# Three banks for the first layer, an ELU with two ScalarE passes, and scores from stacked rounded parts

## The chip, the core and the metric

The kernel runs on one core of one Trainium2 chip. The core has a matrix engine (TensorE, PE in the profile; PEld is its loading of weights), a vector engine (VectorE, DVE), an engine for activation functions (ScalarE, ACT), a general one (GpSimd, POOL), and SyncE (SP), which here issues nearly all DMAs. TensorE writes to PSUM, eight banks of 512 fp32 columns on 128 partitions; the other operands lie in SBUF. The metric is device microseconds of one launch, from inputs in HBM to the output in HBM.

## The reference

Causal block attention (8 batches, 8 heads, 576 positions, head size 64), then a dense layer pair with an ELU, then a soft mixture of eight experts over 32 slots. What matters here is the first two:

```python
scores = scale * np.matmul(q, k.transpose(0, 1, 3, 2))        # 576 x 576 for each of 64 heads
scores = np.where(block_i >= block_j, scores, -1e9)           # blocks of 64 positions
attn = np.exp(scores - np.max(scores, axis=-1, keepdims=True))
attn = attn / (np.sum(attn, axis=-1, keepdims=True) + 1e-09)
x = (attn @ v)                                                # 4608 tokens x 512
h = x @ w_in                                                  # 512 -> 2048
g = np.where(h > 0, h, np.exp(np.minimum(h, 0)) - 1)          # the ELU
y = g @ w_out                                                 # 2048 -> 512
# then: logits = y @ phi; softmax over tokens and over slots; experts on 32 slots; c @ slot_out
```

`w_out` is never applied to the 4608 tokens: it is folded into phi for the logits, and into the 32 slots for the experts.

## The kernel before, in words

**Attention** goes by pairs of heads: 32 pairs, four to a batch. `pair_load` and `pair_prep` bring queries and keys of a pair so that head 0 lies on partitions 0 to 63 and head 1 on 64 to 127, with the 64 head dimensions on the partitions. Pairs below `NTP` = 8 are transposed by TensorE out of a raw load (L516), later ones by VectorE (L525), after which GpSimd scales the queries (L531). `pair_scores` (L552) makes the scores in four fills of two PSUM banks: fill 0 the last 64 queries of both heads, fill 1 the two units of 512 keys, fill 2 those of 384 and 128, fill 3 those of 256. In fills 1 to 3 the two heads are fp32 products on 64 rows of the array each, side by side (L576); an fp32 product shows as two matmuls in the trace. Fill 0 of a later pair is a product on all 128 rows, of queries padded with zeros (L568). VectorE masks (L584) and takes the negated maximum (L587), ScalarE the exp with its sum (L590), GpSimd divides by the sum (L607). From pair 8 on, the weights are transposed by VectorE in 32 x 32 blocks (L689), with the blocks swapped through DRAM by DMAs (L717 to L721), and partly by TensorE through bank PTB (L700). The value products (L739) write banks PTB and PVB, and two copies bring them to the token ring `XR`.

**The first layer** goes by tiles of 128 tokens, 36 of them, each in four ranges of 512 hidden units. `tile_split` splits the tokens in a rounded part and the rest (L793, L795). A range is 12 products of 512 columns into one bank (L808 to L810: high x high, high x low, low x high, for four pieces of 128), alternately banks 0 and 1. ScalarE takes exp(h) into a buffer `E` (L813), VectorE min(e, 1) - 1 (L815), then the maximum with h into a slot of `g` (L818). From there VectorE's block transpose and DMAs turn `g` (`tile_turn`), and `tile_routing` makes the logits (L853) and sums the slots (L919).

**The order** is written by a list scheduler in the program (`Plan`). Every operation has an engine, an assumed duration, the buffers that it reads and writes, and a key; each engine takes the ready operation of the lowest key, at a time that the assumed durations give. DMAs share one modelled queue. The result is a fixed order for each engine. TensorE operations carry a mode (F full array, R row halves, C and D column parts), and a change costs the scheduler 0.13 us. At the end `tail` works the experts off, from pieces of 1 MB that are loaded into places that become free (`slots`).

## Time and profile before

| | us |
|---|---|
| median of 3 runs (lowest, highest) | 956.05 (955.30, 958.82) |
| the profiled execution | 955.77 |
| its span, first to last instruction | 954.0 |
| TensorE busy | 908.7 (95%) |
| VectorE busy | 675.9 (71%) |
| ScalarE busy | 439.4 (46%) |
| GpSimd busy | 272.6 (29%) |

Busy time is the union of an engine's instructions. Matmuls overlap in it, and their ends are modelled, so for TensorE the distance from one start to the next tells more. Idle time has a releaser: the instruction or DMA whose end let the engine go on. The kernel's shape in time: to 85 us attention alone and the splitting of the weights; from 86 to 866 us the first layer's tiles, with attention beside them to 779 us; then the experts and the output.

### The profile page before, as it was taken

How to read it: one execution, taken by the hardware profiler on the slowest of the kernel's cores; microseconds unless marked ns; L12 is line 12 of the kernel's file. 1: busy time of each engine (PE TensorE's matmuls, PEld its weight loads, DVE VectorE, ACT ScalarE, POOL GpSimd, SP SyncE). 2: the span in 40 equal slices, each digit the busy share in tenths (PEclk: the TensorE clock that was granted, in tenths of full speed). 3: DMA queues.
4: the chain of work that ended last, by engine and by line, in shares of the span. 5: the costliest groups of instructions: out<-in, count | busy, mean ns of one | idle time of the engine just before them, and what ended most of it. 6: DMA issues, size and time to landing. Idle time of an engine off the chain costs nothing.

```text
span 954.0 us, 19403 instructions
## 1 busy us (share of the span) xinstructions
PE 908.7 (95%) x6708; PEld 623.3 (65%) x6708; DVE 675.9 (71%) x1718; ACT 439.4 (46%) x1285; POOL 272.6 (29%) x428
## 2 busy tenths in 40 slices
PE   8889999999999999999999999999999999999992
PEld 6556777666666766676766666766776776766350
DVE  5887795668787887777888878887887844333160
ACT  5775655445445535444445445444444333322143
POOL 2863442133342332222323432332332210000000
PEclk9999999999999999999999999999999999999996
DMA  9846755647777785767677777667756498068969
GB/s 235 243 130 171 220 184 159 146 115 207 202 203 218 197 209 184 212 181 211 194 203 206 199 208 201 202 188 203 206 163 217 144 305 340 3 216 298 377 223 342
DMA packets 253217, 197.08 MB, mean 207 GB/s; under 512 B 183232, under 2 KB 206400, under 8 KB 250048
## 3 DMA queue, kind: packets, MB, share of 16 engines
q1 hardware_dynamic: 251920, 195.55, 69.1%
q8 instruction: 54, 0.88, 0.4%
q10 hardware_dynamic: 1200, 0.30, 0.1%
q14 instruction: 43, 0.35, 0.1%
HBM read 125.52 MB, written 70.25 MB: 205 GB/s over the span
## 4 chain that ended last, share of the span: by engine, by line
PE 74%; DVE 8%; DMA 7%; SPq 4%; ACT 2%; issue 2%; POOL 1%; ACTq 0%; DVEq 0%; POOLq 0%
PE ps L808 13%; PE ps L810 11%; PE ps L809 11%; PE ps L360 8%; PE ps L576 7%; PE ps L739 7%; SPq L355 4%; PE ps L919 3%; PE ps L568 2%; PE ps L853 2%; DMA att<-swapped 2%; DMA swapped<-att 2%; PE ps L767 2%; DVE base L587 2%; PE ps L460 1%
## 5 line engine op out<-in xcount | busy, mean ns | idle before, releaser
L808 PE MATMUL ps<-w,xhl 128*128 128x512 f32 x576 | 249.8, 434 | 7.8 <-DVE g L818 5.5
L607 POOL TENSOR_SCALAR att<-att,base 128x128 f32<-128x128 f32 (+4 forms) x288 | 181.0, 647 | 222.2 <-DVE base L603 151.0
L810 PE MATMUL ps<-w,xhl 128*128 128x512 f32 x576 | 226.8, 394 | 0.0
L809 PE MATMUL ps<-w,xhl 128*128 128x512 f32 x576 | 225.7, 392 | 0.0
L590 ACT ACTIVATE att<-ps,base 128x128 f32<-128x128 f32 (+4 forms) x288 | 157.4, 552 | 122.9 <-DVE base L587 121.0
L587 DVE TENSOR_REDUCE base<-ps 128x1 f32<-128x128 f32 (+4 forms) x288 | 135.7, 503 | 21.3 <-PE ps L572 12.2
L808 PEld LDWEIGHTS ps<-w,xhl 128*128 128x128 f32 x576 | 108.8, 189 | 52.0 <-issue 19.1
L813 ACT ACTIVATE xe<-ps 128x512 f32<-128x512 f32 x144 | 86.0, 600 | 115.0 <-PE ps L810 113.7
L810 PEld LDWEIGHTS ps<-w,xhl 128*128 128x128 f32 x576 | 108.1, 188 | 24.9
L336 ACT COPY att<-ps 128x128 f32<-128x128 f32 (+3 forms) x192 | 75.7, 434 | 95.8 <-PE ps L360 90.6
L809 PEld LDWEIGHTS ps<-w,xhl 128*128 128x128 f32 x576 | 108.9, 189 | 14.8
L815 DVE TENSOR_SCALAR xe<-xe 128x512 f32<-128x512 f32 x144 | 68.1, 473 | 67.0 <-ACT xe L813 65.6
L576 PE MATMUL ps<-att 64*128 64x128 f32 (+3 forms) x512 | 96.1, 468 | 1.0 <-ACT att L590 1.0
L360 PE MATMUL ps<-base,att 128*128 128x128 f32 (+1 forms) x496 | 83.2, 282 | 9.7 <-POOL att L607 8.5
L360 PEld LDWEIGHTS ps<-base,att 128*128 128x128 f32 (+1 forms) x496 | 58.0, 143 | 44.5 <-POOL att L607 17.6
L795 POOL TENSOR_TENSOR xhl<-xe,xhl 128x512 fp32r<-128x512 f32 x36 | 46.3, 1291 | 133.1 <-ACT xhl L793 127.0
L818 DVE TENSOR_TENSOR g<-xe,ps 128x512 f32<-128x512 f32 x108 | 73.3, 680 | 2.4
L689 DVE STREAM_TRANSPOSE att<-att 128x384 f32<-128x384 f32 x144 | 70.4, 507 | 5.3 <-POOL att L607 4.2
L739 PE MATMUL ps<-att 128*64 128x64 f32 (+4 forms) x864 | 71.9, 318 | 1.2 <-DMA att<-swapped 0.7
L576 PEld LDWEIGHTS ps<-att 64*128 64x128 f32 x512 | 42.0, 185 | 40.6 <-issue 14.1
L739 PEld LDWEIGHTS ps<-att 128*64 128x64 f32 x864 | 46.8, 137 | 32.3 <-issue 23.6
L826 DVE STREAM_TRANSPOSE g<-g 128x512 f32<-128x512 f32 x84 | 58.0, 695 | 1.7 <-DMA turned<-g 0.2
(134 smaller groups left out, 1115.1 us busy)
## 6 DMA issues: line engine op xcount, KB each, us to landing
turned<-g SPq DMA_DIRECT2D x60, 512.0 KB, 3.1
swapped<-att SPq DMA_DIRECT2D x24, 1024.0 KB, 4.6
g<-turned SPq DMA_DIRECT2D x120, 96.0 KB, 2.6
att<-in_moe_w_dram SPq DMA_DIRECT2D x11, 1024.0 KB, 11.8
att<-swapped SPq DMA_DIRECT2D x48, 192.0 KB, 3.9
att<-in_v_dram SPq DMA_DIRECT2D x64, 128.0 KB, 3.2
g<-in_moe_w_in_dram SPq DMA_DIRECT2D x16, 512.0 KB, 5.3
w_late<-in_moe_w_dram SPq DMA_DIRECT2D x8, 1024.0 KB, 6.9
```

Of the source, the lines that this page charges most:

```text
L336: nc.scalar.copy(o, i)
L360: mm(o, lhsT=i, rhs=f(IDN + base, n, base, base + n), start=True, stop=True, is_transpose=True)
L576: mm(pb(at((u, h)), P * (u + 1)), lhsT=f(qt + P * u, P, 64 * h, 64 * h + 64), rhs=f(kt, P * (u + 1), 64 * h, 64 * h + 64), start=True, sto ...
L587: add("DVE", 0.08 + wide(x) / 960, lambda e, x=x, c=c: nc.vector.tensor_reduce(out=f(c, 1), in_=pb(at(x), wide(x)), axis=AX.X, op=ALU.max, ...
L590: add("ACT", 0.50 + wide(x) / 1300, lambda e, x=x, c=c: nc.scalar.activation(f(pat(x, n), wide(x)), pb(at(x), wide(x)), AF.Exp, bias=f(c, ...
L607: add("POOL", (0.28 + wide(x) / 1050) * (1.3 if n < 8 else 1.0), lambda e, x=x, p=p: nc.gpsimd.tensor_scalar(out=f(p, wide(x)), in0=f(p, w ...
L739: mm(pb(o, w, 64 * h, 64 * h + 64), lhsT=f(vs + 320 * h + D * c, D), rhs=rhs(h), start=start, stop=stop)
L808: mm(pb(bank, 512), lhsT=fr(xh + P * kk, P), rhs=hi, start=(kk == 0), stop=False)
L809: mm(pb(bank, 512), lhsT=fr(xh + P * kk, P), rhs=lo, start=False, stop=False)
L810: mm(pb(bank, 512), lhsT=fr(xl + P * kk, P), rhs=hi, start=False, stop=(kk == 3))
L813: add("ACT", 0.48, lambda e: nc.scalar.activation(f(ee, 512), pb(bank, 512), AF.Exp), r=[("h", hb)], w=[("e", hb)], key=kr)
L818: add("DVE", 0.6, lambda e: nc.vector.tensor_tensor(out=f(g, 512), in0=f(ee, 512), in1=pb(bank, 512), op=ALU.max), r=[("e", hb), ("h", hb) ...
```

## The change

- **Third bank.** In tiles 6 to 33 (`THREE`) the ranges rotate through banks 0, 1 and PTB, and the exp is written into the range's slot of `g` in place of `E`. PTB is freed by letting TensorE's weight transposes use PVB, where the value products follow; their last 64 columns go to the end of the logits' bank (POST + 448), as five products of 64 columns.
- **ELU.** In tiles 6 to 29 (`RELU`) ScalarE takes relu(-h) and then exp(-that); VectorE takes max(e - 1, h) in one instruction, reading `g` and PSUM.
- **Scores.** From pair 9 on (`STACK`) queries and keys are split in a rounded part and the rest. X1 has the rounded queries on both halves of the partitions, X2 the queries' rest on the head's own half and zeros on the other, and Y the rounded keys on the own half and the keys' rest on the other. A unit is X1 by Y plus X2 by Y, both rounded products on the full array (L622 after). The own halves are written by ScalarE (L556, L558) and GpSimd (L567), the other halves come by DMA; the keys' rest is made by GpSimd first (L562). There is one place for queries, keys and stack where queries and keys had two, and masks of fill 2 are two memsets for four. Pair 8 now goes the raw way of the earlier pairs.
- **Tail.** Two of the pieces' places lie in the stack's area, one of them in parts, loaded by four DMAs.

```diff
...
+TLAG, LATE, NTP, JOINED, STACK = 2.5, 30, 8, 5, 9
+THREE = (6, 34)
+RELU = (6, 30)
...
+        if n == STACK:
+        for src, o, nm in ((q, RQ, "rq"), (k, RK, "rk")):
...
+        pair_split(n, key)
...
+    def pair_split(n, key):
+        add("POOL", 0.64, lambda e: nc.gpsimd.tensor_scalar(
+            out=f(QT[0], 512), in0=f(QT[0], 512), scalar1=SCALE, scalar2=0.0, op0=ALU.mult, op1=ALU.add), w=[("qt", 0)], key=key + 0.5)
+        for h in range(2):
+            here, there = (D * h, D * h + D), (D - D * h, P - D * h)
+            x1, x2, y, kl = X1[h], X2[h], Y[h], KL
+
+            def key_of(j):
+                return [("stack", h, j)]
+            add("ACT", 0.5, lambda e, x1=x1, here=here: nc.scalar.copy(st(x1, 512, *here), f(QT[0], 512, *here)),
+                r=[("qt", 0)], w=key_of(0), key=key + 1)
+            add("ACT", 0.5, lambda e, y=y, here=here: nc.scalar.copy(st(y, 512, *here), f(KT[0], 512, *here)),
+                r=[("kt", 0)], w=key_of(1), key=key + 1)
+            load(lambda x1=x1, there=there: st(x1, 512, *there, F32), lambda x1=x1, here=here: st(x1, 512, *here, F32), 200000,
+                 r=key_of(0), w=key_of(2), key=key + 2, lag=TLAG)
+            add("POOL", 1.35, lambda e, y=y, here=here: nc.gpsimd.tensor_tensor(
+                out=st(KL, 512, *here), in0=f(KT[0], 512, *here), in1=st(y, 512, *here, F32), op=ALU.subtract),
+                r=[("kt", 0)] + key_of(1), w=[("kl", h)], key=key + 2)
+            load(lambda y=y, there=there: st(y, 512, *there, F32), lambda here=here: st(KL, 512, *here, F32), 200000,
+                 r=[("kl", h)], w=key_of(3), key=key + 3, lag=TLAG)
+            add("POOL", 1.47, lambda e, x1=x1, x2=x2, here=here: nc.gpsimd.tensor_tensor(
+                out=st(x2, 512, *here), in0=f(QT[0], 512, *here), in1=st(x1, 512, *here, F32), op=ALU.subtract),
+                r=[("qt", 0)] + key_of(0), w=key_of(4), key=key + 3)
...
-        last = fill == 0 and n >= NTP
-        add("PE", (0.0 if last else 0.15) + cols / 600, sc, r=([("qb", s, 0), ("qb", s, 1)] if last else [("qt", s)]) + [("kt", s)], w=bkeys, key=key,
-            load=1.0, mode="F" if last else "R")
+        last = fill == 0 and n >= STACK
+        if n >= STACK and not last:
+            for h in range(2):
+                mine = [u for u, y in units if y == h]
+
+                def st_sc(e, h=h, mine=mine):
+                    for u in mine:
+                        for x, first in ((X1, True), (X2, False)):
+                            mm(pb(at((u, h)), P * (u + 1)), lhsT=st(x[h] + P * u, P), rhs=st(Y[h], P * (u + 1)), start=first, stop=not first)
+                add("PE", sum(2 * (0.016 + P * (u + 1) / 2400) for u in mine), st_sc, r=[("stack", h, j) for j in range(6)], w=[bkeys[h]], key=key)
+        else:
+            add("PE", (0.0 if last else 0.15) + cols / 600, sc, r=([("qb", s, h) for h in range(3)] if last else [("qt", one)]) + [("kt", one)],
+                w=bkeys, key=key, load=1.0, mode="F" if last else "R")
...
+            if n >= STACK and fill == 2 and x[0] == 2:
+                both = pb(at(x) + 256, 256, 0, 64).rearrange("p (a y) -> p a y", a=2)[:, :, 64:]
+                add("DVE", 0.14, lambda e, both=both: nc.vector.memset(both, MASKED), w=keys(x), key=key)
+            elif x != "b" and not (n >= STACK and fill == 2):
...
-            tb, tk = (PTB, "ptb")
+            tb, tk = (PVB, "pvb")
...
-            go(PTB, P, 0, lambda h: both[:, h, 0:P], True, True)
+            go(PVB, P, 0, lambda h: both[:, h, 0:P], True, True)
             for c in range(3):
                 w = P * (4 - max(c, 1))
-                go(PVB + 384 - w, w, c, lambda h: far(h, c), c == 0, False)
-                go(PVB + 384, 64, c, lambda h: both[:, h, P + 64 * c:P + 64 * c + 64], False, False)
-            go(PVB + 256, 192, 3, lambda h: both[:, h, 320:512], False, False)
-            go(PVB + 384, 64, 4, lambda h: both[:, h, 512:576], False, True)
-        add("PE", 3.0, pv, r=[("v", n % NV, j) for j in range(3)] + swap_keys(sl), w=["ptb", "pvb"], key=key, load=0.25, mode="C")
-        add(*evict(n, P), lambda e: copy(e, f(ring, P), pb(PTB, P)), r=["ptb"], w=[("xr", p, b % 2, 0)], key=key)
-        add(*evict(n, 448), lambda e: copy(e, f(ring + P, 448), pb(PVB, 448)), r=["pvb"], w=[("xr", p, b % 2, 1)], key=key)
+                go(PVB + 512 - w, w, c, lambda h: far(h, c), c == 0, False)
+            go(PVB + 384, P, 3, lambda h: both[:, h, 320:448], False, True)
+            for c in range(5):
+                x = P + 64 * c if c < 3 else 64 * c + 256
+                go(POST + 448, 64, c, lambda h: both[:, h, x:x + 64], c == 0, c == 4)
+        add("PE", 3.0, pv, r=[("v", n % NV, j) for j in range(3)] + swap_keys(sl), w=["pvb", "pvx"], key=key, load=0.25, mode="C")
+        add(*evict(n, 512), lambda e: copy(e, f(ring, 512), pb(PVB, 512)), r=["pvb"], w=[("xr", p, b % 2, 0)], key=key)
+        add(*evict(n, 64), lambda e: copy(e, f(ring + 512, 64), pb(POST + 448, 64)), r=["pvx"], w=[("xr", p, b % 2, 1)], key=key)
...
+        three = THREE[0] <= i < THREE[1]
+        if three:
+            hb = (4 * i + r) % 3
+        if (i, r) == (THREE[0], 0):
+            handover([("h", 2)], ["ptb"])
-        bank, ee = H0 + 512 * hb, E + 512 * hb
+        bank, ee, ek = ((H0, H0 + 512, PTB)[hb], g, gk) if three else (H0 + 512 * hb, E + 512 * hb, ("e", hb))
...
-        add("ACT", 0.48, lambda e: nc.scalar.activation(f(ee, 512), pb(bank, 512), AF.Exp),
-            r=[("h", hb)], w=[("e", hb)], key=kr)
-        add("DVE", 0.335, lambda e: nc.vector.tensor_scalar(
-            out=f(ee, 512), in0=f(ee, 512), scalar1=1.0, scalar2=-1.0, op0=ALU.min, op1=ALU.add),
-            w=[("e", hb)], key=kr)
-        add("DVE", 0.6, lambda e: nc.vector.tensor_tensor(
-            out=f(g, 512), in0=f(ee, 512), in1=pb(bank, 512), op=ALU.max),
-            r=[("e", hb), ("h", hb)], w=[gk], key=kr)
+        if RELU[0] <= i < RELU[1]:
+            add("ACT", 0.58, lambda e: nc.scalar.activation(f(ee, 512), pb(bank, 512), AF.Relu, scale=-1.0),
+                r=[("h", hb)], w=[ek], key=kr)
+            add("ACT", 0.55, lambda e: nc.scalar.activation(f(ee, 512), f(ee, 512), AF.Exp, scale=-1.0), w=[ek], key=kr)
+            add("DVE", 0.68, lambda e: nc.vector.scalar_tensor_tensor(
+                out=f(g, 512), in0=f(ee, 512), scalar=-1.0, in1=pb(bank, 512), op0=ALU.add, op1=ALU.max),
+                r=[ek, ("h", hb)], w=[gk], key=kr)
+        else:
+            add("ACT", 0.48, lambda e: nc.scalar.activation(f(ee, 512), pb(bank, 512), AF.Exp),
+                r=[("h", hb)], w=[ek], key=kr)
+            add("DVE", 0.335, lambda e: nc.vector.tensor_scalar(
+                out=f(ee, 512), in0=f(ee, 512), scalar1=1.0, scalar2=-1.0, op0=ALU.min, op1=ALU.add),
+                w=[ek], key=kr)
+            add("DVE", 0.6, lambda e: nc.vector.tensor_tensor(
+                out=f(g, 512), in0=f(ee, 512), in1=pb(bank, 512), op=ALU.max),
+                r=[ek, ("h", hb)], w=[gk], key=kr)
...
-        slots = [(flat(PT + PIECE * j), att) for j in range(10)]
+        slots = [(flat(PT + PIECE * j), att) for j in range(8)]
+        slots += [(lambda: renew("qk", F32, 1)[:, 0:PIECE].rearrange("p (c d) -> p c d", d=512), qkk), (lambda: parted, qkk + att)]
...
+                if o is not parted:
+                    nc.sync.dma_start(out=o.rearrange("p (c f) d -> p c (f d)", f=2) if wide else o,
+                                      in_=src.rearrange("(c p) d -> p c d", p=P))
+                    return
+                for c in range(4):
+                    part = src[P * (c // 2):P * (c // 2) + P, 512 * (c % 2):512 * (c % 2) + 512] if wide else src[P * c:P * c + P, :]
+                    nc.sync.dma_start(out=o[:, c, :], in_=part)
```

Three places in the order. First TensorE, fill 2 of a pair among first-layer products (L808 to L810 before, L862 to L864 after; `w` is the range's weights, `att` and `qk_late` hold queries and keys), before:

```order
L810 MATMUL ps<-w_70,xhl 128x512
L880 MATMUL ps<-base 128x128
L881 MATMUL ps<-base 128x32
L576 MATMUL ps<-att 128x384 x2
L576 MATMUL ps<-att 128x128 x2
L808 MATMUL ps<-w_71,xhl 128x512
L809 MATMUL ps<-w_71,xhl 128x512
L810 MATMUL ps<-w_71,xhl 128x512
L360 MATMUL ps<-base 128x128
```

and after:

```order
L862 MATMUL ps<-w_71,xhl 128x512
L863 MATMUL ps<-w_71,xhl 128x512
L864 MATMUL ps<-w_71,xhl 128x512
L622 MATMUL ps<-qk_late_2028 128x384 x2
L622 MATMUL ps<-qk_late_2028 128x128 x2
L862 MATMUL ps<-w_68,xhl 128x512
L863 MATMUL ps<-w_68,xhl 128x512
L864 MATMUL ps<-w_68,xhl 128x512
L369 MATMUL ps<-base 128x128
```

Two fp32 units of both heads have become, for one head, two rounded products of 384 and two of 128; the other head's stand a few products on.

Second ScalarE, at fills 2 and 3 of a pair (L590 and L638 are the scores' exp, L813 the ELU's), before:

```order
L590 ACTIVATE att,base<-ps,base 128x384
L590 ACTIVATE att,base<-ps,base 128x128 x2
L813 ACTIVATE xe<-ps 128x512 x2
L590 ACTIVATE att,base<-ps,base 128x256 x2
L813 ACTIVATE xe<-ps 128x512
L793 CAST xhl<-xe 128x512
L590 ACTIVATE att,base<-ps,base 128x576
```

and after:

```order
L870 ACTIVATE att<-att 128x512
L638 ACTIVATE att,base<-ps,base 128x384
L638 ACTIVATE att,base<-ps,base 128x128 x2
L868 ACTIVATE att<-ps 128x512
L556 CAST qk_late_2028<-att 64x512
L558 CAST qk_late_2028<-att 64x512
L638 ACTIVATE att,base<-ps,base 128x256 x2
```

The ELU has its two passes (L868 from PSUM, L870 in place), and two casts of the next pair's stack (L556, L558) stand ahead of fill 3's exps; two more follow.

Third GpSimd, from a pair's queries to its weights (L607 and L655; the 384, 128 and 256 columns are the second half), before:

```order
L607 TENSOR_SCALAR att<-att,base 128x576
L607 TENSOR_SCALAR att<-att,base 128x512 x2
L528 TENSOR_SCALAR base<-att 64x64 x2
L531 TENSOR_SCALAR att<-att 128x512
L607 TENSOR_SCALAR att<-att,base 128x384 x2
L607 TENSOR_SCALAR att<-att,base 128x128 x2
L607 TENSOR_SCALAR att<-att,base 128x256 x2
L795 TENSOR_TENSOR xhl<-xe,xhl 128x512
```

and after:

```order
L536 TENSOR_SCALAR att<-att 64x64 x2
L548 TENSOR_SCALAR att<-att 128x512
L655 TENSOR_SCALAR att<-att,base 128x576
L655 TENSOR_SCALAR att<-att,base 128x512 x2
L567 TENSOR_TENSOR qk_late_2028<-att,qk_late_2028 64x512
L562 TENSOR_TENSOR qk_late_2028<-att,qk_late_2028 64x512 x2
```

Between a pair's two halves of weights now stand the four subtractions of the next pair's stack (the fourth, L567, is the next row), and the second half comes behind them.

## Rows read from the trace of the kernel before

**Rows 1.** The page, part 1: busy us, share of the span, instructions.

```profile
PE 908.7 (95%) x6708; PEld 623.3 (65%) x6708; DVE 675.9 (71%) x1718; ACT 439.4 (46%) x1285; POOL 272.6 (29%) x428
```

**Rows 2.** Windows: stretch, length, busy us (instructions), TensorE clock, DMA share, GB/s.

```profile
165.00:866.00 701.00, 690.42 (x4936) 479.92 (x4924) 523.38 (x1371) 309.27 (x957) 194.24 (x329) 1.00 0.68 197
866.00:954.00 88.00, 66.37 (x575) 32.83 (x574) 26.17 (x52) 27.00 (x56) 0.00 (x0) 0.91 0.85 312
```

**Rows 3.** TensorE's waits, 200 to 760 us: us, times, longest us.

```profile
PE ps L808 <- DVE g L818: 5.5, 6, 2.0
...
PE ps L808 <- DVE att L818: 2.2, 3, 1.0
...
PE ps L739 <- DMA g<-turned: 0.4, 2, 0.2
```

**Rows 4.** TensorE's timeline: start us, us, line, operation, shape, count.

```profile
303.19 0.40 PE L810 MATMUL ps<-w,xhl 128*128 128x512 f32 x1
303.51 0.70 PE L576 MATMUL ps<-att 64*128 64x256 f32 x4
304.15 2.95 PE L739 MATMUL ps<-att 128*64 128x128 f32 x36
307.03 0.50 PE L808 MATMUL ps<-w,xhl 128*128 128x512 f32 x1
...
308.26 1.14 PE L568 MATMUL ps<-att,base 128*128 128x288 f32 x4
...
318.83 1.14 PE L576 MATMUL ps<-att 64*128 64x384 f32 x8
319.90 0.50 PE L808 MATMUL ps<-w,xhl 128*128 128x512 f32 x1
320.24 0.40 PE L809 MATMUL ps<-w,xhl 128*128 128x512 f32 x1
320.47 0.39 PE L810 MATMUL ps<-w,xhl 128*128 128x512 f32 x1
320.70 0.60 PE L360 MATMUL ps<-base,att 128*128 128x128 f32 x4
...
321.38 0.40 PE L809 MATMUL ps<-w,xhl 128*128 128x512 f32 x1
...
326.43 0.70 PE L576 MATMUL ps<-att 64*128 64x256 f32 x4
...
334.63 1.13 PE L576 MATMUL ps<-att 64*128 64x512 f32 x4
335.69 2.95 PE L739 MATMUL ps<-att 128*64 128x128 f32 x36
```

**Rows 5.** Instructions by line and form: busy us, mean ns, idle before and releasers.

```profile
L813 ACT ACTIVATE xe<-ps 128x512 f32<-128x512 f32 x144 | 86.0, 600 | 115.0 <-PE ps L810 113.7
...
L818 DVE TENSOR_TENSOR g<-xe,ps 128x512 f32<-128x512 f32 x108 | 73.3, 680 | 2.4
...
L815 DVE TENSOR_SCALAR xe<-xe 128x512 f32<-128x512 f32 x144 | 68.1, 473 | 67.0 <-ACT xe L813 65.6
...
L924 DVE SCALAR_TENSOR_TENSOR base<-base,ps 128x512 f32<-128x512 f32 x34 | 25.0, 737 | 13.4 <-PE ps L919 13.2
...
L793 ACT CAST xhl<-xe 128x512 fp32r<-128x512 f32 x36 | 22.0, 621 | 3.0 <-DVE xe L338 2.9
```

**Rows 6.** Timeline at 834 us, GpSimd and VectorE.

```profile
834.03 1.30 POOL L795 TENSOR_TENSOR xhl<-xe,xhl 128x512 fp32r<-128x512 f32 x1 [14.31 <-ACT xhl L793]
...
834.49 1.12 DVE L815 TENSOR_SCALAR xe<-xe 128x512 f32<-128x512 f32 x1 [2.50 <-ACT xe L813]
```

**Rows 7.** DMA issues: KB each, median us from issue to landing.

```profile
turned<-g SPq DMA_DIRECT2D x60, 512.0 KB, 3.1
...
g<-turned SPq DMA_DIRECT2D x120, 64.0 KB, 2.4
```

**Rows 8.** Waits of SyncE's queue: us, times, longest us.

```profile
SPq L355 <- DVE g L826: 32.8, 15, 6.5
```

More of the change, by code (lines that the diff above doesn't have):

```diff
@@ L258, in attention_moe_kernel @@
     SM = base.take(144)
-    QB = base.take(2 * P)
     XR = xe.take(4 * RING)
@@ L280, in attention_moe_kernel @@
     PB = aa.take(2 * PW[0] + PW[1])
+    X1, X2, Y, KL = (0, 512), (1024, 1536), (2048, 2560), 3072
+    qa.take(KL + 512 - qa.size)
     XH = xa.take(2 * 512)
@@ L391, in zero @@
                 nc.gpsimd.memset(f(PB + PW[0] * s + S, 64), 0.0)
-            nc.gpsimd.memset(f(QB, 2 * P), 0.0)
             for s in range(NV):
                 nc.gpsimd.memset(f(V + 640 * s, 640, 64, P).rearrange("p (h x) -> p h x", h=2)[:, :, 256:320], 0.0)
-        add("POOL", 0.9, zero, w=[("p", "b", s) for s in range(2)] + [("v", s, 2) for s in range(NV)] +
-            [("qb", s, h) for s in range(2) for h in range(2)], key=k0)
+        add("POOL", 0.9, zero, w=[("p", "b", s) for s in range(2)] + [("v", s, 2) for s in range(NV)], key=k0)
         raws = [(G + 1024 * j, 512, [("g", 2 * j), ("g", 2 * j + 1)]) for j in range(3)] + \
@@ L479, in pair_load @@
         b, p = divmod(n, 4)
-        s = n % 2
-        if n < NTP:
+        if n < STACK:
             for j, src in enumerate((q, k)):
@@ L531, in pair_prep @@
-        add("POOL", 0.55, lambda e: nc.gpsimd.tensor_scalar(
-            out=f(QT + S * s, 512), in0=f(QT + S * s, 512), scalar1=SCALE, scalar2=0.0, op0=ALU.mult, op1=ALU.add),
-            w=[("qt", s)], key=key + 1)
+                out=f(QB + P * s + D * h, D, D * h, D * h + D), in0=f(QT[0] + 512, D, D * h, D * h + D),
+                scalar1=SCALE, scalar2=0.0, op0=ALU.mult, op1=ALU.add), r=[("qt", 0)], w=[("qb", s, h)], key=key + 3.5)
+        if n == STACK:
+            handover([("stack", h, j) for h in range(2) for j in range(6)], [("qt", 1), ("kt", 1)] + [("raw", x, h) for x in range(3) for h in range(3)])
+            for h in range(2):
+                add("POOL", 0.4, lambda e, h=h: nc.gpsimd.memset(st(X2[h], 512, D - D * h, P - D * h, F32), 0.0), w=[("stack", h, 5)], key=key - 20)
@@ L564, in sc @@
         def sc(e):
-            if fill == 0 and n >= NTP:
+            if fill == 0 and n >= STACK:
                 for y in range(2):
@@ L1177, in attention_moe_kernel @@
     ev = []
+    before = None
     for n in range(NPAIR):
```

70 lines of the change are left out of this document (41 added, 29 removed).

## The prediction

> **What bounds the kernel now.** I read the views from the whole to the part. The busy totals first: TensorE works 908.7 of 954.0 us, VectorE 71%, ScalarE 46%, GpSimd 29% [rows 1]. Then two stretches: from 165 to 866 us TensorE is busy 690 of 701 us at a granted clock of 1.00, the higher of its two levels; the last 88 us are another regime, TensorE 66 us busy and the DMA engines at 0.85 [rows 2]. In the first stretch VectorE is the next engine, 523 of 701, ScalarE 309, GpSimd 194. Then the waits: between 200 and 760 us TensorE stood still mostly because a first-layer bank was not yet read, 5.5 + 2.2 us [rows 3]. So in the long stretch the time is TensorE's list, end to end, and only what shortens that list, or the 7.7 us of waits, counts. Busy time alone hides how it is spent, since ends of matmuls are modelled and overlap; I take distances from one start to the next in the timeline [rows 4].
>
> There a first-layer product of 512 rounded columns takes 0.23 us (320.24 to 320.47). Where a score block of two 64-row halves follows, the last product takes 0.32 (303.19 to 303.51): 0.09 more at the way in. The blocks themselves take 1.06 us (the two 512-column units, 334.63 to 335.69), 1.07 (384 and 128, 318.83 to 319.90) and 0.64 (256, 303.51 to 304.15). The first product behind one takes 0.34 (319.90 to 320.24): 0.11 more at the way out. Four 128-column transposes with the product behind them take 0.68 (320.70 to 321.38); less 0.23, that is 0.11 each, not a quarter of 0.23: so narrow a product does not go at its columns' price.
>
> **Scores.** Pairs 9 to 31, 23 of them, change. A pair now pays 1.06 + 1.07 + 0.64 = 2.77 us, and 3 x 0.09 on the way in, 3.04. The stacked form needs per unit two full-array rounded products: 4 of 512 columns, 4 of 384, 4 of 128, 4 of 256. No row shows 384 or 256 rounded columns: bounded below by columns (0.23 x 384/512 = 0.17 and 0.115), above by the 0.23 of a 512 product. I take the lower ends, because 512 columns are the same kind of product and nearest, and 0.11 for 128 from the transposes: 4 x (0.23 + 0.17 + 0.11 + 0.115) = 2.5 us. Saved 0.54 x 23 = 12.4 us. The way out of 0.11 goes too where a first-layer product follows, in half of the 69 blocks (38 of 77 in the order of before): 3.8 us. Value products and logits have array shapes of their own; where they stood beside a score block one change of shape served both, which now is paid to the first layer: I give 2 us back. The ends: every narrow product at 0.23 makes the pair 16 x 0.23 = 3.68, a loss of 0.64 x 23 = 14.7 us; columns alone (5,120 x 0.23/512 = 2.3) and a way out of 0.11 at every block a gain of 1.07 x 23 = 24.6 us.
>
> The 64-row blocks run both heads side by side. The Trainium skill (TensorEngine Tiling (Array Packing), Theoretical Speedup) gives up to a factor of two for that when a dimension is at most 64; by it alone, giving the packing up would cost another 2.77 us per pair, some 64 us, and the sum would be near 1003. The rows speak against it here: one fp32 512-column unit costs half of 1.06, two rounded products 0.46.
>
> **Third bank.** The 5.5 + 2.2 us of TensorE's waits for VectorE's last read of a bank [rows 3] should go between tiles 6 and 33. The stretch holds 34 tiles of four ranges, 5 us a range, and a bank will have two other ranges in which to be read, where it had one. I take 6 us; ends 0 and 7.7. Late next are the value products, which wait for the DMA that swaps the weights' blocks.
>
> **ELU.** Tiles 6 to 29, 96 ranges: ScalarE runs two passes (0.60 each by its Exp) where it ran one, +58 us; VectorE loses a pass of 0.47, and its last one becomes a form like the accumulation's 0.74 for 0.68: -0.41 x 96 = -40 us [rows 5]. The stacks add four casts of 0.62 a pair on ScalarE (+57 us) [rows 5] and four subtractions of 1.30 on GpSimd (+120 us) [rows 6]. ScalarE then has 309 + 115 = 424 of 701, GpSimd 314, VectorE 483: all under TensorE's 690, so I price them at nothing. The cover is the distance between a range and its bank's next use; gone, each range would pay the added pass, 0.6 x 96 = 58 us.
>
> **Stack.** Pair n+1's parts can be written only when pair n's last score block has read them, and its first stacked block waits for them, with the first layer queued behind it on TensorE. GpSimd takes the four subtractions in the order queries, keys, keys, queries, the first after two casts: the second half's keys are done after 2 x 0.62 + 3 x 1.30 = 5.1 us and then copied, 128 KB, for 2.4 to 3.1 us by the nearest copies [rows 7]: 7.5 to 8.2 us. In the order of after some 21 first-layer products (4.8 us), the 128-row block (1.1 at 308.26) and the value products (2.88, 304.15 to 307.03) stand between, 8.8 us; for other pairs as much in first-layer products. Before, the places stood 8.2 us apart (326.43 to 334.63) [rows 4]. So there is 0.6 to 1.3 us of room. The nearest wait, that of the value products for copied blocks, is 0.4 us in the whole stretch [rows 3]: I take 1 us, the upper end is a rival. GpSimd's weights of a pair's second half now stand behind the subtractions, so the value products' data come up to 5.2 us later; in the order the value products stand later too.
>
> **The rest.** Pair 8 goes the earlier pairs' way: ten transposes, +1.1 us. Value products get one more product of 64 columns for the same 1,600 columns: between 0 and 2.88/36 x 4 = 0.32 a pair, 7.4 us; equal columns are nearer, so 1 us. Transposes and values now share one bank; that they take turns there is as it was in the bank they leave. The tail (pieces in other places, one in four DMAs) moves with the last tile; between -2 and +2, taken 0.
>
> Sum: -12.4 - 3.8 + 2 - 6 + 1 + 1.1 + 1 = -17 us. The profiled execution took 955.77, so 939 (the median is 956.05, 0.3 more).
>
> **Rivals.** *The stack copy is late (slower).* The four copies stand in SyncE's one queue, among copies that wait for VectorE's transposes 2.2 us a time (32.8 us in 15) [rows 8]. With one such wait ahead of every pair's last copy, less 0.8 us of room, TensorE stands 1.4 us a pair: 23 x 1.4 = 32 us, so 971; from 17/23 = 0.74 us a pair the gain is gone. For it: path and room differ by little. Against: value products behind that same queue hardly wait now. 0.14.
>
> *VectorE takes TensorE's place (no change).* Beside a GpSimd subtraction the pass that goes took 1.12 us where its mean is 0.47 [rows 5, 6]. If 92 more subtractions hold other passes as long, VectorE has 92 x 0.65 = 60 us more, 543 of some 685, in bursts that TensorE waits for, and what the list loses comes back: 956. The Trainium skill (SBUF — State Buffer, Who interferes with whom) says that a VectorE instruction in a two-port mode, or with two SBUF inputs, excludes one of GpSimd for its whole length, and that one with at most one SBUF input outside those modes doesn't. The row agrees for the pass that goes; by that rule the new last pass, with one input in PSUM, is free, which no row here shows. 0.09.
>
> *More goes than I count.* The columns' end of the scores, -24.6, all 7.7 us of waits, and nothing new: 955.8 - 32 + 3 = 926. For it: every change of shape shows at both sides. Against: narrow products don't go by columns. 0.13.
>
> *It doesn't do what it says.* The waits for banks stay, because VectorE reads a bank as late as before (523 of 701 us busy), and value products and stacks pay 4 us more than taken: 955.8 - 12.4 - 3.8 + 2 + 1.1 + 6 = 949. 0.09.
>
> **Numbers.** Forecast 939, own range 931 to 947, 0.55; more gain 0.13; scores alone 0.09; no change 0.09; slower 0.14. Faster by over 0.5% (under 951.3; about what can be told from no change) takes the first three, 0.77. For eight in ten I go from 925, past the larger gain, to 954, which leaves out the slower case.
>
> **What would show it.** Right: TensorE's list from the first tile's steady pace to the last range about 17 us shorter, a stacked block of 512 columns with 0.23 us from start to start and no longer product before it, waits of the first layer for VectorE near zero, ScalarE up by 115 us and VectorE down by 40. Wrong: TensorE waiting at the first stacked block for a copy or for GpSimd, 128- and 256-column stacked products at 0.2 us, or VectorE's other passes longer. If TensorE's busy share falls below 0.95 in the long stretch, the forecast is wrong in kind and not in size.

## The result: slower by 1.4%

The changed kernel took 969.11 us (median of 4 runs, 967.96 to 971.93), the kernel before beside it 955.67 (954.39 to 958.82): ratio 1.0135, 95% interval 1.0105 to 1.0166. The forecast was 939, so it failed by 30 us and in sign. The profiled execution has a span of 967.6 us, 13.6 more than before.

The busy line of the page, and the two stretches (the second is again the tail):

```profile
PE 903.2 (93%) x6817; PEld 655.0 (68%) x6817; DVE 648.1 (67%) x1583; ACT 553.0 (57%) x1469; POOL 384.7 (40%) x519
```

```profile
165.00:880.00 715.00, 686.72 (x5060) 512.91 (x5058) 497.56 (x1236) 423.04 (x1141) 305.59 (x422) 1.00 0.74 209
880.00:967.00 87.00, 66.43 (x575) 32.84 (x574) 26.16 (x52) 26.83 (x56) 0.00 (x0) 0.91 0.87 315
```

Against [rows 1, 2]: ScalarE +114 us, GpSimd +112, VectorE -28 (counted: -40); the tail as long as before. All of the loss is in the long stretch, where TensorE works 4 us less in 14 us more: 0.96 of the time. TensorE's waits there (200 to 775 us) answer to [rows 3]:

```profile
PE ps L787 <- DMA att<-swapped: 9.8, 7, 3.3
PE ps L369 <- ACT base L951: 6.1, 4, 2.1
PE ps L622 <- DMA qk_late<-qk_late: 3.3, 3, 1.7
PE ps L862 <- DVE g L871: 2.0, 2, 1.2
PE ps L915 <- DMA g<-turned: 1.8, 3, 1.1
PE ps L787 <- DMA g<-turned: 1.2, 2, 0.7
```

The bank waits of the first layer (L862) fell from 7.7 us to 2.0: the third bank works. In their place, for one, the value products (L787) wait for the copy that brings the weights' swapped blocks back (att<-swapped), which was no row of weight before. The stack's own copies (L622 <- qk_late) take 3.3 us, not 32. The transposes' wait for ScalarE's exponential of the dispatch (L369 <- base L951) is new as well.

Where the time stands I took from the distance of each TensorE product's start to the next, from the first first-layer product to the last, summed by line; a wait counts to the product ahead of it (us):

| | before | after | no_copies (below) |
|---|---|---|---|
| first layer | 439.8 | 431.5 | 435.4 |
| value products, pairs 8 to 31 | 71.4 | 91.7 | 74.6 |
| score blocks, 128 columns and more | 80.6 | 76.8 | 74.8 |
| transposes | 54.8 | 57.3 | 54.2 |
| routing logits | 27.7 | 29.9 | 27.6 |
| all else | 105.8 | 106.9 | 104.7 |
| sum | 780.1 | 794.2 | 771.4 |

A value block without a wait takes 2.89 us (2.88 before, 4 products fewer). Of the 24 blocks' 91.7 us 22 are therefore lost, more than the whole loss of 14. By my sums these are three things. In 9 blocks TensorE stops behind the first four products until the swapped blocks have landed: 12.5 us (2.0 before). In two of them, pairs 14 and 22, the granted clock then stands at 0.50, the lower of its two levels, for 3.4 us, and the products come at half their pace: 3.0 us (none before).

```profile
381.30:384.70 3.40, 3.40 (x12) 1.60 (x14) 0.48 (x2) 0.00 (x0) 0.76 (x2) 0.50 0.61 159
579.30:582.70 3.40, 3.40 (x32) 2.68 (x28) 0.38 (x2) 0.58 (x1) 2.08 (x5) 0.50 0.39 105
```

And 6.5 us (0 before) are not the value products' at all: in 4 blocks they stand behind the last product, where a dispatch transpose waits for ScalarE, and count to the value block only because a wait counts to the product ahead of it. Pair 18:

```profile
479.21 2.96 PE L787 MATMUL ps<-att 128*64 128x128 f32 x40
484.29 0.33 PE L369 MATMUL ps<-base 128*128 128x128 f32 x1 [2.11 <-ACT base L951]
```

The longest stall for the swapped blocks, pair 14. First the place on TensorE:

```profile
377.22 0.40 PE L864 MATMUL ps<-w,xhl 128*128 128x512 f32 x1
377.54 0.44 PE L787 MATMUL ps<-att 128*64 128x128 f32 x4
381.28 4.42 PE L787 MATMUL ps<-att 128*64 128x384 f32 x36 [3.30 <-DMA att<-swapped]
385.62 1.08 PE L915 MATMUL ps<-g,base 128*32 128x128 f32 x32
```

8.08 us from 377.54 to 385.62 for a block of 2.89, 3.5 of them the stop and 1.7 the clock. Then SyncE's queue for the same pair, before and after (start, time of the issues, tiles, count; swapped<-att is the way out, att<-swapped the way back):

```profile
357.88 0.37 SPq L355 DMA_DIRECT2D swapped<-att  x1
358.30 3.06 SPq L355 DMA_DIRECT2D g<-turned  x4
361.40 0.42 SPq L355 DMA_DIRECT2D att<-in_k_dram  x1
362.34 3.28 SPq L355 DMA_DIRECT2D att<-swapped  x6
```

```profile
355.24 0.82 SPq L364 DMA_DIRECT2D qk_late<-qk_late  x1
356.11 2.94 SPq L364 DMA_DIRECT2D g<-turned  x6
359.14 1.11 SPq L364 DMA_DIRECT2D qk_late<-qk_late  x2
360.37 2.31 SPq L364 DMA_DIRECT2D att<-in_q_dram  x4
362.78 0.44 SPq L364 DMA_DIRECT2D turned<-g  x1
363.31 0.51 SPq L364 DMA_DIRECT2D att<-in_v_dram  x1
363.91 0.74 SPq L364 DMA_DIRECT2D swapped<-att  x1
364.75 1.61 SPq L364 DMA_DIRECT2D att<-in_v_dram  x2
366.45 4.30 SPq L364 DMA_DIRECT2D att<-in_k_dram  x4
370.80 2.84 SPq L364 DMA_DIRECT2D g<-turned  x6
373.74 0.37 SPq L364 DMA_DIRECT2D turned<-g  x1
374.15 3.18 SPq L364 DMA_DIRECT2D att<-swapped  x6
```

Read the gaps: after, there are none. GpSimd ended this pair's last weights at 357.3 (L655, 354.56 and 2.75 us) and VectorE their last block transpose at 358.8 (L737); the way out was issued at 363.91, behind the tile's blocks, stack copies and the next pair's queries, landed at 370.7, and the way back was issued at 374.15, behind keys and the tile's blocks. Before, the way back followed the way out's landing at once. Summed over the rows of 215 to 765 us, the queue's issues take 377 of 550 us before and 462 after: +57 for the 92 stack copies, and the loads beside them a little longer each.

### The profile page after: what moved, and what is told of

Same layout as the page of the kernel before. It is cut to its first block, busy times and chain, and to the rows that moved or that the text cites. A ratio compares the mean times of both kernels' runs of the same rounds, so it can differ in the third digit from the quotient of the medians.

```text
span 967.6 us, 20058 instructions
## 1 busy us (share of the span) xinstructions
PE 903.2 (93%) x6817; PEld 655.0 (68%) x6817; DVE 648.1 (67%) x1583; ACT 553.0 (57%) x1469; POOL 384.7 (40%) x519
## 4 chain that ended last, share of the span: by engine, by line
PE 59%; DMA 12%; DVE 7%; SPq 7%; ACT 6%; POOL 4%; issue 3%; ACTq 0%; DVEq 0%; POOLq 0%
PE ps L862 10%; PE ps L863 9%; PE ps L864 9%; PE ps L369 7%; SPq L364 7%; PE ps L787 5%; PE ps L622 4%; POOL att L655 3%; PE ps L981 2%; DMA att<-swapped 2%; PE ps L915 2%; DMA qk_late<-qk_late 2%; PE ps L816 2%; PE ps L611 2%; ACT att L638 2%
## 5 line engine op out<-in xcount | busy, mean ns | idle before, releaser
L655 POOL TENSOR_SCALAR att<-att,base 128x128 f32<-128x128 f32 (+4 forms) x288 | 179.7, 642 | 201.1 <-DVE base L651 113.8
L862 PE MATMUL ps<-w,xhl 128*128 128x512 f32 x576 | 246.6, 428 | 2.0 <-DVE g L871 2.0
L864 PE MATMUL ps<-w,xhl 128*128 128x512 f32 x576 | 226.6, 393 | 0.6 <-POOL xhl L844 0.6
L638 ACT ACTIVATE att<-ps,base 128x128 f32<-128x128 f32 (+4 forms) x288 | 157.5, 551 | 85.3 <-DVE base L635 76.0
L635 DVE TENSOR_REDUCE base<-ps 128x1 f32<-128x128 f32 (+4 forms) x288 | 139.4, 506 | 22.2 <-PE ps L607 10.5
L862 PEld LDWEIGHTS ps<-w,xhl 128*128 128x128 f32 x576 | 108.9, 189 | 33.7 <-issue 11.9
L864 PEld LDWEIGHTS ps<-w,xhl 128*128 128x128 f32 x576 | 108.1, 188 | 25.9 <-POOL xhl L844 1.2
L345 ACT COPY att<-ps 128x512 f32<-128x512 f32 (+3 forms) x184 | 73.0, 437 | 67.9 <-PE ps L369 62.5
L567 POOL TENSOR_TENSOR qk_late<-att,qk_late 64x512 fp32r<-64x512 f32 x46 | 59.0, 1283 | 90.7 <-ACT qk_late L556 64.3
L787 PE MATMUL ps<-att 128*64 128x128 f32 (+2 forms) x960 | 76.1, 312 | 11.5 <-DMA att<-swapped 9.8
L622 PE MATMUL ps<-qk_late 128*128 128x512 f32 (+3 forms) x368 | 77.6, 328 | 4.5 <-DMA qk_late<-qk_late 3.3
L369 PE MATMUL ps<-base,att 128*128 128x128 f32 x416 | 69.9, 280 | 10.6 <-POOL att L655 9.8
L787 PEld LDWEIGHTS ps<-att 128*64 128x64 f32 x960 | 50.3, 141 | 41.9 <-issue 30.9
L622 PEld LDWEIGHTS ps<-qk_late 128*128 128x128 f32 x368 | 61.3, 188 | 21.3 <-issue 6.9
L369 PEld LDWEIGHTS ps<-base,att 128*128 128x128 f32 x416 | 49.1, 143 | 39.2 <-POOL att L655 16.9
L737 DVE STREAM_TRANSPOSE att<-att 128x384 f32<-128x384 f32 x144 | 68.6, 503 | 1.0 <-POOL att L655 0.8
L562 POOL TENSOR_TENSOR qk_late<-att,qk_late 64x512 fp32r<-64x512 f32 x46 | 59.1, 1285 | 4.2 <-ACT qk_late L558 2.8
L638 ACT ACTIVATION_READ_ACCUMULATOR att<-ps,base 128x1 f32 x288 | 57.4, 199 | 0.0
```

The source lines that it names most:

```text
L345: nc.scalar.copy(o, i)
L369: mm(o, lhsT=i, rhs=f(IDN + base, n, base, base + n), start=True, stop=True, is_transpose=True)
L622: mm(pb(at((u, h)), P * (u + 1)), lhsT=st(x[h] + P * u, P), rhs=st(Y[h], P * (u + 1)), start=first, stop=not first)
L635: add("DVE", 0.08 + wide(x) / 960, lambda e, x=x, c=c: nc.vector.tensor_reduce(out=f(c, 1), in_=pb(at(x), wide(x)), axis=AX.X, op=ALU.max, ...
L638: add("ACT", 0.50 + wide(x) / 1300, lambda e, x=x, c=c: nc.scalar.activation(f(pat(x, n), wide(x)), pb(at(x), wide(x)), AF.Exp, bias=f(c, ...
L655: add("POOL", (0.28 + wide(x) / 1050) * (1.3 if n < 8 else 1.0), lambda e, x=x, p=p: nc.gpsimd.tensor_scalar(out=f(p, wide(x)), in0=f(p, w ...
```

## Experiments

Times are medians; "before" is what ran beside them, 955.2 to 957.0. Theory Q is SyncE's queue, G the subtractions on GpSimd, S ScalarE's second pass, B the bank that transposes and values share, T the copies' bytes, P the price of any other written-out order. The values' last 64 columns (line 795 of after) lie in the routing's bank, and a slot sum of one of the first five tiles fills all 512 columns of that bank; no dependence keeps the two apart, in the changed kernel neither. Its order does (pair 9's values from 262.4 us, VectorE's read of the sum at 261.8). In copies_act, after_lag, q_act, q_act_elu and no_copies one pair's values come over such a sum before it is read (no_copies: sum from 255.95, values from 256.95, the read at 259.95), in no_sub and rows3 a sum over values, so what they compute is not the reference's. It is one place near 250 us and every instruction is issued, so the times are read; with the two kept apart the order, and with it the time, would be another.

**Which part of the change.** Scores as before (the diff's other parts kept):

> Third bank, the value products' new places and the ELU as in the changed kernel; scores as before, so no casts, no subtractions, no stack copies. Theory Q (SyncE's queue is full, and the weights' copies for the value products wait in it): value products wait as little as before (2 to 4 us in all), the first layer keeps its 8 us: 946 to 950. Theory G (the subtractions on GpSimd hold up the weights): the same 946 to 950, since they are gone as well. Theory S (ScalarE's second pass of the ELU is what makes the chain late): 956 or more, with value products waiting.

Measured 964.68, ratio 1.0093 (1.0061 to 1.0126). Theories Q and G had 946 to 950 and fail; S had 956 or more with value products waiting, and 8 us are lost, 6 of them in value products. But bank_only below, without S's second pass, is as slow.

The stack copies on ScalarE:

```
-    r=key_of(0), w=key_of(2), key=key + 2, lag=TLAG)
+    r=key_of(0), w=key_of(2), key=key + 2, lag=TLAG, eng="ACT")
```

> The changed kernel with its 92 stack copies issued by ScalarE in place of SyncE; the same bytes at about the same times. Theory Q: 57 us of issue time leave SyncE's queue (92 x 0.62), the 20 us that TensorE loses in the value products fall under 8, 952 to 958. Theory G: nothing changes for GpSimd, 965 to 971. Theory S: ScalarE gets more to do, 972 or more. If the transfers themselves and not the queue are what is slow, 965 to 971 too.

Measured 1116.28, far beyond the 972 that theory S named: TensorE waits 51.7 us for the swapped blocks and 36.6 for the tile's. As I read it, without a run for it: a copy that waits for a subtraction now stands in ScalarE's order among its casts, exponentials and evictions. The run says nothing on Q.

No subtractions (their two instructions removed, low parts zeroed once):

> The changed kernel without its 92 subtractions: the low parts of queries and keys are set to zero once, so the scores are the rounded products alone; casts and stack copies stay. Theory G: GpSimd loses 118 us, the weights of a pair's second half come 5 us earlier, the value products' waits fall under 5 us, 948 to 953. Theory Q: the copies still stand behind the same loads, and the waits keep half or more: 960 to 968. Theory S: 966 to 971.

Measured 969.14, no change, with 115 us less on GpSimd than after:

```profile
PE 906.0 (94%) x6817; PEld 656.5 (68%) x6817; DVE 627.1 (65%) x1582; ACT 554.7 (57%) x1470; POOL 269.7 (28%) x428
```

GpSimd's weights come 2 us earlier (below), and by starts the value products take 7.3 us less (84.4 for 91.7); but routing takes 7.3 more (37.2 for 29.9), waiting for the tile's blocks. So G has a share in the value products' waits, and in this order nothing of it shows in the time.

```profile
PE ps L910 <- DMA g<-turned: 7.5, 5, 2.9
```

The ELU as before, `RELU = (6, 6)`:

> The changed kernel with the ELU of before (one pass of ScalarE, two of VectorE), the third bank kept. Theory S: ScalarE loses 58 us, the waits in the value products fall, 955 or less. Theories Q and G: neither queue nor GpSimd changes, 966 to 972, and VectorE's 40 us more may add a little.

Measured 963.72, ratio 1.0074 (1.005 to 1.0098): 5.4 us less, between the theories. That is no more than another order alone will be seen to move the kernel before, so it is not shown to be the second pass.

**Each part alone.** `RELU = (6, 6)` in no_stack; then `THREE = (6, 6)` in no_stack; then both in the changed kernel:

> Third bank and the value products' new places alone; ELU and scores as before. Theory S (ScalarE's second pass of the ELU makes the chain late): the 8 us that the three parts of the last runs lost (third bank, places, ELU together 964.7) are the ELU's, so 948 to 953, the first layer 5 to 8 us shorter. Theory B (transposes and value products that share one bank, or the exponential written straight into the hidden tile, hold each other up): 958 to 965.

> The new ELU and the value products' new places, two banks, scores as before. Theory S: 960 to 966, with TensorE waiting for ScalarE's exponentials of scores and routing. Theory B: 954 to 958, VectorE's 40 us less being of no use to a list that TensorE bounds.

> Stacked scores and the value products' new places; two banks, ELU as before. Theory Q (SyncE's queue holds the weights' copies back): 958 to 964, value products waiting 10 to 15 us, and the first layer waiting 8 us for banks as before. Theory S: with no second pass of the ELU the stack is harmless: 948 to 955.

Measured 965.14, 969.09 and 974.01 (ratios 1.0102, 1.016, 1.0188). The first is at the upper end of theory B's range, the other two are over all that I had named. Each alone is slower than before, and the three together are not the sum of them. The new ELU is worth 0 without the stack (964.68 and 965.14). What the three share are the value products' new places, so these alone (`RELU` and `THREE` both (6, 6) in no_stack), and beside them the kernel before with a number of its planner changed, first `TLAG` 2.5 to 3.5, then `EARLY` 16 to 15, which adds and takes no instruction:

> Of the change only this: transposed weights and value products share one bank, the values' last 64 columns lie in another, 40 products for 36. ELU, scores and the number of first-layer banks as before. Theory B (the shared bank holds the attention chain up, and that is why each part alone was 9 to 18 us slower, since all three had it): 963 to 968. Theory P (the written-out order of before is a lucky one, and any other order loses about 10 us, whatever the edit): 955 to 968, with no wait that stands out at the shared bank. Neither: 955 to 957, and third bank, ELU and stack each cost by themselves.

> The kernel before with one number of its planner changed: copies are assumed to land 1 us later (3.5 for 2.5), no instruction is added or taken. Theory P: the order changes and 5 us or more are lost, 961 to 968. Theory B: the assumption comes nearer to the 3.1 to 5 us that the trace shows, 952 to 958.

> The kernel before with another number of its planner (pairs come up to 15 us ahead of their tiles, where it was 16), no instruction added or taken. Theory P (the order of before is a lucky one): 959 to 966 again, as with the copies' assumed time. Without P: 954 to 958, and then the 6 us of the other run were that assumption's own.

Measured 962.03 (1.0046 to 1.0091), 963.45 (1.003 to 1.0097) and 961.96 (1.0048 to 1.0097): 5 to 7 us three times, for different reasons to reorder. P stands, and B, though not excluded, is not needed. TensorE's waits show what the order of before had spared, here before_lag, to be read against [rows 3]:

```profile
PE ps L808 <- DVE g L818: 7.7, 8, 1.8
PE ps L808 <- DVE att L818: 3.1, 5, 1.0
```

10.8 us for 7.7; by starts the first layer takes 447.3 for 439.8. With a third bank the order's price falls elsewhere: in bank_only the first layer is at 435.9, and transposes wait for ScalarE's exponentials of the dispatch instead.

```profile
PE ps L362 <- ACT base L905: 4.9, 3, 3.4
PE ps L816 <- DVE g L834: 2.0, 1, 2.0
```

**SyncE's queue.** The stack copies removed (both `load` calls of pair_split; the halves zeroed once):

> The changed kernel without its 92 stack copies: the halves of the stacks that they fill are set to zero once, so the scores lack the products with low parts; casts, subtractions, ELU and third bank stay. Theory Q: 57 us of issue leave SyncE's queue, the weights' copies start 3 us earlier after the way out, value products lose under 8 us where they lost 20: 954 to 960. Theory S: 964 to 969, and the waits are for ScalarE or behind it.

Measured 947.75, ratio 0.9922 (0.9896 to 0.9947): 21.4 us under the changed kernel and under the kernel before, with casts, subtractions, ELU and third bank all in place, more than theory Q asked. This kernel, too, has an order of its own. Of the value products' 22 us 5 are left, 1 of them for their copies:

```profile
PE ps L369 <- ACT base L949: 3.8, 4, 1.9
PE ps L620 <- ACT att L636: 3.4, 5, 1.6
...
PE ps L785 <- DMA att<-swapped: 0.5, 1, 0.5
```

The same copies at one eighth of the width from pair 10 on, with every instruction in its place on every engine:

```
-    st(x1, 512, *there, F32), ... st(x1, 512, *here, F32), 200000,
+    st(x1, 512 if n == STACK else 64, *there, F32), ... st(x1, 512 if n == STACK else 64, *here, F32), 200000,
```

> The changed kernel with every instruction and wait in its place on every engine, but the stack copies of pairs 10 to 31 carry 64 columns for 512 (the rest of a stack keeps what pair 9 left there). Theory Q (it is the 92 issues in SyncE's queue): little changes, 963 to 971, and the weights' copies still start some 4 us after they could. Theory T (it is the copies' bytes, 11.8 MB, beside the other transfers): 948 to 956. The order is the same, so the price of another order has no part in it.

Measured 961.89, ratio 1.0062 (1.0043 to 1.0081): 7 of the 21 us. Neither theory alone. The orders are the same and 10.1 MB are left out, so the bytes are a third of it: a copy lands in 2.45 us for 3.15 in the median, and by starts the value products take 3.4 us less, the transposes (ahead of stack blocks) 3.2, routing 2.3. The value products still lose 19 us where they lost 22: the stops for the swapped blocks fell from 12.5 to 8.9, the 6.5 behind the last product stayed.

The planner told the truth (`TLAG` 3.5, 0.62 us an issue for 0.48):

> The changed kernel whose planner assumes 3.5 us for 2.5 until a copy lands and 0.62 us for 0.48 of SyncE's time for each issue, as the trace has them. Theory Q: the planner now sees the queue fill, puts the value products later and something else in front, the stalls of 20 us in them fall to under 8: 953 to 960. If the queue can't be hidden by any order, since the loop from scores to copies is itself too long: 964 or more.

Measured 972.82, as in the second case (964 or more). The value products' loss does fall, from 22 to 12 us, but the first layer starts at 93.1 us for 85.6, and from there on 4 us are won (790.1 for 794.2): no gain from truer assumptions, and not every microsecond that value products wait is one of the kernel's.

Queries loaded by ScalarE, in the changed kernel and in the one before:

```
-    w=[(nm, a)], key=key, eng=queue(n))
+    w=[(nm, a)], key=key, eng="ACT" if nm == "rq" else "SP")
```

> The changed kernel with the 92 loads of raw queries issued by ScalarE in place of SyncE; nothing else, and the stack copies stay on SyncE. Theory Q (92 issues too many in SyncE's queue): as many issues leave the queue as the stacks brought, some 55 us; the value products lose under 10 us where they lost 20: 948 to 960, if ScalarE has room for 92 x 0.47 us of issue. Theory T (it is not the issue but the copies' traffic, or GpSimd and ScalarE's work for the stacks): 965 to 971.

> The kernel before with its loads of raw queries from pair 8 on issued by ScalarE, the control: its SyncE queue was busy 377 of 550 us and its value products lost 2 us. Theory Q: nothing to win there, 955 to 963 (up to 6 of it the price of another order, as with the copies' assumed time). If it falls under 952, SyncE's queue already bounded the kernel before, and the stack is not needed to explain what the runs show.

Measured 1015.76 and 993.6, and 1035.36 with the old ELU (q_act_elu, for which I expected 944 to 955). Wrong all three, and the control shows that the move itself costs 38 us. In q_act SyncE's queue now waits for the other queue's loads:

```profile
SPq L364 <- DMA att<-in_q_dram: 89.4, 32, 8.5
```

The Trainium skill (DMA: Bandwidth & Descriptors, Issuing engines are not separate DMA queues) says that starting transfers from several engines saves only the sequencer's time, usually small beside the transfer. These runs cannot test that, since the move cost more than such time could give back; beside a stack copy's 3.15 us to landing its issue of 0.62 us is a fifth.

**Rounded scores without a copy.** High and low parts stay in their head's rows; three products of 64 rows a unit, high x high, high x low, low x high, the heads side by side:

```
-  mm(..., lhsT=st(x[h] + P * u, P), rhs=st(Y[h], P * (u + 1)), start=first, stop=not first)
+  mm(..., lhsT=st(x + P * u, P, *rows), rhs=st(y, P * (u + 1), *rows), start=(x, y) == (X1, Y), stop=x == X2)
```

> The changed kernel without stacks: the rounded and the low parts stay in the rows of their head (two casts and two subtractions of 128 rows a pair, no copy), and a score block takes three rounded products of 64 rows (high x high, high x low, low x high), the two heads beside each other. Third bank, places, ELU as in the changed kernel. Theory Q: without the copies the queue is as in no_copies, 948 or less; if the heads' products run beside each other as the fp32 ones do, a pair's scores take 3 x 1,280 columns x 0.23/512 = 1.7 us and 0.6 of mode changes for 2.7: 925 to 945. Theory B: the shared bank's 10 us stay in that, so not under 935. If 64-row rounded products don't run side by side: 3.5 us a pair and 965.

Measured 949.93, ratio 0.9923 (0.9904 to 0.9942), above the expected 925 to 945, and with the one place of values and slot sums left out of order, as said above. The heads do run side by side: six products of 512 columns in 0.90 us, the other two blocks 1.00 and 0.55.

```profile
402.39 0.97 PE L606 MATMUL ps<-qk_late 64*128 64x512 f32 x6 [0.23 <-ACT att L622]
403.29 0.50 PE L846 MATMUL ps<-w,xhl 128*128 128x512 f32 x1
...
407.07 1.07 PE L606 MATMUL ps<-qk_late 64*128 64x384 f32 x12
408.07 0.66 PE L369 MATMUL ps<-base,att 128*128 128x128 f32 x4
...
416.43 0.62 PE L606 MATMUL ps<-qk_late 64*128 64x256 f32 x6
416.98 0.50 PE L846 MATMUL ps<-w,xhl 128*128 128x512 f32 x1
```

With the next pair's transposes held behind these products (`+ [("qt", 0), ("kt", 0)]` in what they read):

> As rows3 (three rounded products of 64 rows a score unit, the two heads beside each other, no stack and no copy; third bank, places and new ELU as in the changed kernel), with a pair's products added to what the next pair's transposes of queries and keys wait for. Theory Q: no copies, so 948 to 954, under both kernels; the added wait costs nothing as long as transposes, casts and subtractions (5.5 us) fit before the next pair's products. If they don't: 955 to 962, with TensorE waiting for the subtractions.

Measured 969.2, ratio 1.0129. The expectation failed: no copy, a queue with room, and 19 us more than rows3. Against rows3, by starts, transposes take 4.9 us more, the first layer 4.3, routing 4.2, value products 3.0; one routing block waits 3.9 us until 782.6 us, in the only 50 us window of the long stretch whose granted clock is under 1.00 (at 0.50 for 10.2 us from 781.5 and 3.4 from 795.1; an estimate from these is 6 of the 19 us):

```profile
765.00:815.00 50.00, 43.55 (x354) 29.81 (x353) 19.36 (x51) 14.55 (x40) 5.26 (x8) 0.86 0.82 292
```

So even without copies one wait, and the order that it makes, decide over as much as taking the copies out won.

## Why the prediction was wrong

The path from a pair's last score block to its value products, in means over pairs 9 to 30 (my sums from the traces, us):

| | before | after | no_sub | narrow_copies | no_copies | rows3 |
|---|---|---|---|---|---|---|
| last scores to last weight (GpSimd) | 6.9 | 8.5 | 6.4 | 8.5 | 8.6 | 7.4 |
| to the issue of the way out | 2.3 | 4.8 | 5.2 | 3.7 | 2.6 | 2.1 |
| to its landing | 4.9 | 5.2 | 4.7 | 5.1 | 4.8 | 4.7 |
| to the issue of the way back | 1.2 | 4.4 | 2.9 | 4.4 | 4.1 | 2.7 |
| to the last landing | 6.1 | 6.3 | 6.5 | 6.3 | 6.3 | 6.5 |
| sum | 21.4 | 29.1 | 25.6 | 28.0 | 26.3 | 23.4 |
| last scores to value products, TensorE | 25.2 | 30.4 | 27.1 | 29.9 | 28.9 | 26.0 |
| lost in value products, 22 pairs | 1.1 | 22.4 | 13.4 | 19.0 | 5.0 | 4.5 |
| of it behind the last product | 0.0 | 6.5 | 3.4 | 6.5 | 4.1 | 3.1 |

Before, the path had 3.8 us of room; after, 7.7 us were added to it and 1.3 of room were left in the mean; 9 of the 24 value blocks stopped for their copies. Of the 7.7, GpSimd has 1.6; of the 2.5 to the way out VectorE's block transposes have 1.1 (2.1 us for 1.0) and SyncE's queue 1.4; ahead of the way back the queue has 3.2. But this last part is 4.1 us without any stack copy, too: it belongs to the order of the queue more than to the 92 issues. What no_copies wins on the path is ahead of the way out (2.6 for 4.8).

- **The step that failed is "Stack".** It asked in SyncE's queue only whether the stack's copies come in time. They nearly do (3.3 us of waits, taken 1). What four more issues a pair, and another order, do to the copies behind them was not asked. "The value products' data come up to 5.2 us later; in the order the value products stand later too": data 7.7 later, products 5.2, and mostly for the queue, where I had it all for GpSimd. A wait priced at nothing cost 10.4 us more than before in stops and 3.0 at the lower clock.
- **The slower rival** (971, 0.14) had the right queue and the wrong victim: not the stack blocks (3.3 us for its 32) but the value products. That its time is nearly the measured one is luck. Its "against", that value products hardly wait in that queue now, was read off [rows 3] as safety; it was 3.8 us of room in the mean.
- **Scores**: mis-sized. These blocks of after answer to [rows 4]:

```profile
336.46 1.17 PE L622 MATMUL ps<-qk_late 128*128 128x512 f32 x4
337.56 2.96 PE L787 MATMUL ps<-att 128*64 128x128 f32 x40
...
342.32 1.36 PE L622 MATMUL ps<-qk_late 128*128 128x384 f32 x8
343.52 0.45 PE L862 MATMUL ps<-w,xhl 128*128 128x512 f32 x1
...
348.29 0.64 PE L622 MATMUL ps<-qk_late 128*128 128x256 f32 x4
348.77 0.40 PE L862 MATMUL ps<-w,xhl 128*128 128x512 f32 x1
```

  1.20 for 384 and 128 (priced 1.12; where one head's stand alone, 0.52 for 0.56), 0.48 for 256 (0.46), 1.10 for 512 ahead of a change of shape, 1.01 in the median (0.92). Over all 23 pairs, waits inside the blocks included, a pair took 2.73 us (priced 2.5) where it had taken 2.90 (2.77): -3.8 us for 6.2. The way in, 0.09 at each of 69 blocks in the sum, another 6.2, was paid only where a first-layer product stands ahead: 5.1 us at 53 blocks before, 0.8 at 68 after, without the waits for stacks. From start to start a second product of 256 columns followed in 0.118 us, one of 128 in 0.06: narrow rounded products do go at nearly their columns' price.
- **Third bank and way out** (-6 and -3.8, less 2): right. Between two first-layer products 6.7 us went; behind score blocks the way out took 2.5 us for 4.2. The first layer's 8.2 us in the table hold these and the way in, less 3.4 us of waits for stacks ahead of their blocks and small terms elsewhere.
- **ELU at nothing**: 5.4 us beside the stack, none without it, and no more than a reordering. The cover that I named, range to next use, held (L862 waits 2.0 us). Two things were not covered: the path above (with the old ELU it is 27.7 us for 29.1, and value products lose 14.5 for 22.4), and the dispatch's exponential on ScalarE, 6.5 us behind value blocks where before there were none. I had priced ScalarE's work at nothing because ScalarE is under TensorE's busy time; that step failed too. What makes this exponential late stays open: with the old ELU 5.9 us stand there, without the copies 4.1.
- **Value products' extra product**: taken 1 us, measured 0.01 us a block.
- **What the sum left out**: that TensorE's order is written out anew by the planner. Three reorderings with no work to speak of cost 5 to 7 us each; the sum had no term for it. How much of the 14 us is such a price, the runs do not tell.
- The named sign, a busy share under 0.95, could not tell: 0.96 with the stalls in it.

So it is shown where the time is lost, and that the copies' bytes have 7 us of it in an unchanged order. Not settled: how the 14 us that remain between narrow_copies and no_copies divide between the 92 issues and the order, since the two kernels are ordered differently; and whether rounded scores in their rows beat the kernel before with the routing's bank held apart from the value products: rows3_held's order keeps them apart and is slower than before, and no run adds that dependence alone.

## What to carry to other kernels

Ask of every added transfer not only when it lands but what stands behind it in its queue, and how much room those have: a wait of 0.4 us in the profile can mean 4 us of room or none. Look at which product a wait stands ahead of before you give it to one. Where the order is a planner's, time two or three reorderings that change no instruction first; a change must beat their spread. A copy that only feeds a shape (full rows) is worth comparing with products that need no copy; here the comparison stays open, since the two orders of rows3 lie 19 us apart.

## What the runs showed of the hardware

- An issue in SyncE's queue took 0.49 us in the mean for blocks (g<-turned, 300 of them) and 0.62 to 0.68 for stacks and loads; in after its issues took 0.84 of the time from 215 to 765 us.
- Rounded products of 64 rows run beside each other in the array: 0.90 us for six of 512 columns, where four of 128 rows take 1.01.
- One 3.9 us wait of TensorE until 782.6 us (rows3_held) went with a granted clock of 0.86 in its 50 us window, all others from 165 to 865 us being at 1.00. In after the clock stood at 0.50 for 3.4 us twice, in value blocks that had just stopped for 3.5 and 2.2 us, and gave 1.7 and 1.3 us away there; the trace of before has no such stretch between 165 and 865 us.
